# A joint unit order for the first batch and the front of the second in a fused retention and Fourier-mix kernel

## The chip, the cores and the metric

The kernel runs on one core of a Trainium2 chip. A core has five engines that run their own instruction streams and meet at semaphores: PE (TensorE, matrix products into PSUM), DVE (VectorE), ACT (ScalarE), POOL (GpSimd) and SP (SyncE, which here only issues DMA transfers). POOL also issues transfers, on a queue of its own that can convert fp32 to fp16. The metric is the device time of one execution in microseconds (us), as the median of several executions.

## The reference

Two layers follow one another. The first is a retention recurrence for 4 batches, 8 heads, 768 steps and head size 64; the second mixes the result with a two-dimensional Fourier transform and runs a normed MLP of width 2048.

```
for t in range(S):
    state = gamma * state + k[t] (outer) v[t]      # per batch and head
    y[t] = scale * q[t] @ state
x = y as (B, S, H * D)                             # 4 x 768 x 512
X = fft(fft(x, axis=1), axis=2)
u = x + real(X)
un = (u - mean(u)) / sqrt(var(u) + 1e-6)           # per row
out = u + relu(un @ w_ch1) @ w_ch2                 # 512 -> 2048 -> 512
```

## The kernel before

One batch after another goes through the same stages. The front of a batch is attention, folds, the two transform stages and the norm; its main part is the MLP.

*Attention.* The recurrence is cut into 6 chunks of 128 steps, and the heads are taken in four pairs. For a pair, q and k are cast to fp16 (k with its decay factor), transposed on PE, multiplied chunk by chunk to masked products (tile `atm`), and k with v gives chunk states (`s16`) that are chained on DVE. Output `y` is the masked product times v plus q times the state before the chunk; it is written to `x16` in fp16. For the first batch these are the small units `q0_unit` (L449), `kl_unit` and `vl_unit` (k and v loads on POOL's queue, L457 and L464), `k0_unit` (L472), `t0_unit` and `te_unit` (transposes and their copies), `am_unit` and `ae_unit` (products on PE, mask on DVE, L515 and L530), `kv0_unit`, `sc_unit`, `yi_unit`, `yx_unit` and `x0_unit`. For later batches larger units do the same: `cast_unit` (L414), `t_unit`, `a_unit`, `kv_unit` and `y_unit`, each with its matmuls and its evictions in one unit.

*Transform.* The sums and differences of mirrored rows and columns (`fold_s` L730, `fold_d` L747, `fold_e`) halve the work; stage 1 (`ps1`, `psA`, `psB`) multiplies by cosine and sine tables over the steps, stage 2 (`pq`) over the 512 features. For the first three row blocks of the first batch, `s2e_unit` (L958) works on PE with x added by `px_unit`; all other blocks go through `s2_unit` (L1025): products, a copy `qn` on ACT, two DVE combinations into `u`, two additions of x on POOL (L1072, L1074), row statistics on DVE (L1085) and the normed `un` on ACT (L1087). `unT_unit` transposes `un` on PE, for later batches by DMA.

*MLP.* 16 column blocks of the first product (`h_unit`, L1126; relu on ACT for the rows named in `ACT_ROWS`, else on DVE) are kept in `ht16` for 384 rows at a time; `ch_unit` (L1170) forms three blocks of 128 output rows from them, 16 matmuls each, and writes `out`. For the first 384 rows of the first batch, `h0_unit` (L1136, matmul L1143) does the first product in 12 groups of 16 matmuls of 128 columns.

*Loads.* SP issues four q loads at the start. The k and v loads of the first batch, the eight weight loads (`w1_unit`, `w2_unit`, 512 KB each in fp16) and the v loads of the second batch are issued by POOL. The second batch's q and k loads (`load_unit`, L163) are issued by SP with two added waits: for the seventh weight load (`w_dma[6]`) and for the last matmul of the eighth `h0_unit` (`lb[0]["mm"]`).

*Order.* `first_units` is a list written out by hand. Its units are emitted one by one, and `pin` ties every instruction to the one before it on its engine, so each engine runs them in list order. All that follows, from the second half of the first batch on, is given to `emit` (L1239) as streams of units with due times (`DM0`, `TS0`, `DA0`, `LD0` for the first batch, `DM1`, `TS1`, `DA1`, `LD1` for the others, in units of one batch); units are emitted by due time, and a planner may then move instructions on an engine, except that up to due time 0.05 all engines and up to 1.0 POOL are pinned, and that nothing up to 1.0 goes ahead of the hand-made list (`behind`). `filler(n)` puts n matmuls on PE whose result is not used.

Of the kernel before, what the change touches and what calls it, by code (L numbers as in the profile page):

```python
# [18 lines left out]
P = 128  # L19
# [11 lines left out]
LOADS = (('q', 0), ('q', 1), ('q', 3), ('q', 2))  # L31
# [3 lines left out]
DM0, DM1 = (0.120, 0.208, 0.265, 0.344), (0.004, 0.137, 0.232, 0.341)  # L35
TS0 = (0.249, 0.368, 0.406, 0.410, 0.479, 0.544, 0.680, 0.685)
# [3 lines left out]
HT0 = (0.655, 0.675, 0.673, 0.628)  # L40
NPE = 2
ACT_ROWS = ((2, 5, 6, 7, 8, 9, 10, 14), (0, 3, 6, 7, 9, 10, 11, 12, 14, 15), (2, 4, 5, 6, 7, 8, 10, 14))
# [3 lines left out]
def kernel(  # L46
# [116 lines left out]
    def load_unit(b, i, after=None):  # L163
        def run():
            h0 = 2 * PAIR_ORDER[i]
            for name, src in srcs.items():
                if b == 1 and name == "v":
                    continue
# [3 lines left out]
                dma = nc.sync.dma_start(t, src[b, h0:h0 + 2].rearrange(rows, p=P))  # L172
                if after is not None:
                    for x in (w_dma[after].ins, lb[0]["mm"].ins):
                        tc.add_manual_dep(dma.ins, x.name,
                                          mybir.DependencyInfo(mybir.DependencyClass.Sync,
                                                               mybir.DependencyReason.DATA),
                                          reason="loads in turn")
# [96 lines left out]
    def late_consts():  # L275
        with tc.issue_after(lb[0]["una"].ins):
            for h in range(H):
                nc.scalar.activation(maskp[:, h // 2, h % 2], maskf, AF.Copy, bias=0.0,
                                     scale=float(gam[h] ** (-P)))

# [26 lines left out]
    def eng_of(eng):  # L307
        return nc.vector if eng == "V" else nc.gpsimd
# [295 lines left out]
    def t_unit(b, i):  # L604
        def run():
            st = at[b, i] = {}
            kT = st["kT"] = tp.tile([P, NCH, P], f16, tag="kT", name="kT")
            if b >= NPE:
                qT = st["qT"] = qts[i % 2]
                nc.sync.dma_start_transpose(qT.rearrange("p h c t -> p (h c) t"),  # L610
                                            q16_of[b, i].rearrange("p h c d -> p (h c d)"))
                nc.sync.dma_start_transpose(kT, kd_of[b, i].rearrange("p c h d -> p (c h d)"))
                return
            qT = st["qT"] = qts[i % 2] if b else qts[i % 2][:, 0]
            for dst, src in ((qT, q16_of[b, i]), (kT, kd_of[b, i])):
                tq = ps_g.tile([P, NCH, P], f16, tag="g", name="tq", padded_shape=[P, 8, P])
                for c in range(NCH):
                    nc.tensor.transpose(tq[:, c, :], src[:, c].rearrange("p a b -> p (a b)"),
                                        ident16)
                if dst is qT:  # L620
                    for h2 in range(2 if b else 1):
                        rows = slice(D * h2, D * h2 + D) if b else slice(0, P)
                        dst = qT[rows, h2] if b else qT
                        (nc.scalar.copy if h2 == 0 or ON_ACT["q"][min(b, 2)] else nc.vector.tensor_copy)(
                            dst.rearrange("p c t -> p (c t)").rearrange(
                                "p (t c) -> p t c", c=NCH),
                            tq[rows].rearrange("p c t -> p t c"))
                else:
                    nc.scalar.copy(dst, tq)
        return run  # L630

    def a0_unit(b, i, half):
        def run():
            st = at[b, i]
            hp = PAIR_ORDER[i]
            if half == 0:
                st["atm"] = ap_.tile([P, NCH, 2, P], f16, tag="atm", name="atm")
            wk = [ps_g.tile([P, 3, P], f32, tag="g", name="wkA", padded_shape=[P, 4, P])
                  for _ in range(2)]
            for c3 in range(3):  # L640
                c = 3 * half + c3
                for h2 in range(2):
                    sl = slice(D * h2, D * h2 + D)
                    nc.tensor.matmul(wk[h2][:, c3, :], st["kT"][sl, c, :], st["qT"][sl, c, :],
                                     start=True, stop=True)
            for h2 in range(2):
                nc.vector.scalar_tensor_tensor(
                    out=st["atm"][:, 3 * half:3 * half + 3, h2, :], in0=wk[h2],
                    scalar=float(gam[2 * hp + h2] ** (-P)),
                    in1=maskf.unsqueeze(1).to_broadcast([P, 3, P]),  # L650
                    op0=ALU.mult, op1=ALU.mult)
        return run
# [483 lines left out]
    def h0_unit(kb, g):  # L1136
        def run():
            unT = lb[0]["unT"]
            psh = ps_pm.tile([P, 4, P], f32, tag="pm", name="psh0")
            for f in range(4):  # L1140
                fb = 4 * g + f
                for cb in range(4):
                    mm = nc.tensor.matmul(psh[:, f], w116[:, cb, fb * P:(fb + 1) * P],  # L1143
                                          unT[:, cb, kb * P:(kb + 1) * P],
                                          start=(cb == 0), stop=(cb == 3))
            lb[0]["n"] = lb[0].get("n", 0) + 1
            if lb[0]["n"] == 8:
                lb[0]["mm"] = mm
            dst = ht16[:, 4 * g:4 * g + 4, kb * P:(kb + 1) * P]
            if g % 2 == 0:  # L1150
                nc.scalar.activation(dst, psh, AF.Relu, bias=0.0, scale=-1.0)
            else:
                nc.vector.tensor_scalar(out=dst, in0=psh, scalar1=-1.0, scalar2=0.0,
                                        op0=ALU.mult, op1=ALU.max)
        return run

# [82 lines left out]
    def emit(streams):  # L1239
# [16 lines left out]
    late_consts()  # L1256
    streams = []
    for b in range(B):
        majors = []
# [64 lines left out]
```

## Time and profile before

| | us |
|---|---|
| median of 3 runs (251.27 to 251.73) | 251.46 |
| the profiled execution's own time | 250.45 |
| its span, first to last instruction | 248.7 |
| PE busy | 236.4 |
| DVE busy | 175.7 |
| ACT busy | 120.9 |
| POOL busy | 91.1 |
| last matmul ends, last store follows | 245.6 |

The profile records each instruction of one execution. A group of equal instructions stands as line, engine, operation, output<-inputs, shape and count, followed by the time that its engine sat idle before it and what ended that idle time. The page also cuts the span into 40 slices of 6.2 us each, in which a digit is the busy share in tenths, and lists the granted clock of PE in the same way. Windows views give busy times for any stretch. Waits views sum the idle time by who waited for whom. The chain of waits follows the last instruction back to what released it. Three more readings: 29 fillers (L156) run between 1.3 and 20.3 us; the transfers of the second batch's k took 10.84 us in that chain; weight loads landed 5.3 to 14.7 us after their issue.

### The profile page before, as it was taken

Reading aid. Unit: us, or ns where it says so; the run is one execution under the profiler, and the core shown is the slowest. Engines: PE = TensorE matmul, PEld = TensorE weight load, DVE = VectorE, ACT = ScalarE, POOL = GpSimd, SP = SyncE. Lnnn points to the kernel's source line nnn. Section 1 sums busy time; section 2 is a strip of 40 time slices with the busy share of each in tenths; the row PEclk is TensorE's granted clock in tenths of the full one; section 3 lists DMA queues with packets and bytes.
Section 4 is the critical chain, followed back from the end, with each engine's and each line's share of the span. In section 5 each row is a group of like instructions: output and inputs, shape, how many; then the busy total and the mean of one; then the engine's idle time right before and its main releaser. Section 6 shows DMA issues by size and latency. Waiting matters only on the chain.

```text
span 248.7 us, 5403 instructions
## 1 busy us (share of the span) xinstructions
PE 236.4 (95%) x2082; PEld 147.6 (59%) x2082; DVE 175.7 (71%) x420; ACT 120.9 (49%) x272; POOL 91.1 (37%) x152
## 2 busy tenths in 40 slices
PE   7897999996999997999999999999999999999994
PEld 2464999743766554665567546655567455445543
DVE  8999645688899878997787647896995747424112
ACT  7886564639686355563237523741248317202500
POOL 8999493154600037782000454780001305000000
PEclk9999599999999999999999999999999999999999
DMA  7999099999769314997989068997200241221012
GB/s 194 182 149 153 2 176 190 187 192 280 252 159 278 72 46 103 234 214 153 244 221 252 8 122 232 208 202 162 87 0 3 44 148 25 44 84 42 3 42 84
DMA packets 99210, 34.04 MB, mean 137 GB/s; under 512 B 89840, under 2 KB 96240, under 8 KB 99184
## 3 DMA queue, kind: packets, MB, share of 16 engines
q1 hardware_dynamic: 76336, 27.14, 45.8%
q0 software_dynamic: 22848, 6.55, 25.4%
q8 instruction: 16, 0.26, 0.4%
q14 instruction: 10, 0.08, 0.1%
HBM read 27.26 MB, written 6.29 MB: 135 GB/s over the span
## 4 chain that ended last, share of the span: by engine, by line
PE 69%; DVE 11%; POOL 8%; DMA 4%; ACT 3%; issue 3%; SPq 1%; POOLq 0%; ACTq 0%
PE psc L1170 26%; PE psh L1126 23%; DMA k<-in_k_dram 4%; PE psh L1143 4%; DVE atm L533 3%; PE wkA L662 3%; PE ps L873 2%; PE wkY L716 2%; PE wkY L712 2%; SPq L172 1%; POOL u L1074 1%; POOL u L1072 1%; DVE xab L741 1%; DVE bst L1085 1%; DVE u L1051 1%
## 5 line engine op out<-in xcount | busy, mean ns | idle before, releaser
L1170 PE MATMUL psc<-w,ht 128*128 128x512 f16 (+2 forms) x400 | 88.1, 370 | 0.0
L1126 PE MATMUL psh<-unT,w 128*128 128x384 f16 x448 | 83.1, 326 | 0.4 <-ACT ht L1130 0.2
L1170 PEld LDWEIGHTS <-ht 128*128 128x128 f16 x400 | 37.8, 98 | 37.9
L1126 PEld LDWEIGHTS <-w 128*128 128x128 f16 x448 | 42.1, 98 | 23.8 <-issue 1.5
L1072 POOL TENSOR_TENSOR u<-u,x 128x256 f32<-128x256 f32 x21 | 13.3, 635 | 106.6 <-DVE u L1051 93.3
L1130 ACT ACTIVATE ht<-psh 128x384 f16<-128x384 f32 x64 | 30.8, 490 | 42.1 <-PE psh L1126 41.6
L1174 DVE SCALAR_TENSOR_TENSOR ob<-psc,stats,u 128x512 f32<-128x512 f32 (+2 forms) x25 | 18.0, 725 | 27.0 <-PE psc L1170 26.5
L1132 DVE TENSOR_SCALAR ht<-psh 128x384 f16<-128x384 f32 x48 | 26.3, 550 | 7.9 <-PE psh L1126 7.5
L1087 ACT ACTIVATE un<-u,stats 128x512 f16<-128x512 f32 x21 | 15.1, 721 | 22.6 <-DVE stats L1086 14.8
L665 DVE TENSOR_TENSOR atm<-wkA,maskp 128x512 f16<-128x512 f32 x36 | 23.9, 684 | 2.5 <-PE wkA L662 2.5
L1085 DVE BATCH_NORM_STATS2 bst<-u 128x6 f32<-128x512 f32 x21 | 14.6, 694 | 8.8 <-POOL u L1074 8.6
L691 DVE SCALAR_TENSOR_TENSOR s<-s,gk,wkK 128x128 f16<-128x128 f16 x48 | 16.2, 338 | 2.2 <-ACT s L687 1.6
L724 ACT ACTIVATE x<-wkY,gexp 128x384 f16<-128x384 f32 x24 | 12.7, 580 | 6.3 <-PE wkY L716 6.1
L435 POOL TENSOR_SCALAR kd<-k,gexp 128x384 f16<-128x384 f32 x24 | 13.8, 585 | 4.7 <-DMA k<-in_k_dram 4.7
L1074 POOL TENSOR_TENSOR u<-u,x 128x256 f32<-128x256 f32 x21 | 13.3, 635 | 3.0 <-DVE u L1054 1.8
L662 PE MATMUL wkA<-qTz,kT 128*128 128x256 f16 x72 | 13.3, 273 | 0.1
L1046 ACT COPY qn<-pq 128x128 f32<-128x128 f32 x18 | 4.9, 273 | 13.2 <-PE pq L1044 12.6
L1143 PE MATMUL psh<-unT,w 128*128 128x128 f16 x192 | 11.2, 219 | 0.0
L156 PE MATMUL wps<-ht 128*128 128x512 f16 x29 | 10.0, 491 | 1.3 <-DVE ht L217 1.3
L1051 DVE SCALAR_TENSOR_TENSOR u<-pq,g,qn 128x256 f32<-128x256 f32 x18 | 8.5, 473 | 3.6 <-PE psh L1126 2.5
L1143 PEld LDWEIGHTS <-w 128*128 128x128 f16 x192 | 10.9, 98 | 0.1
L662 PEld LDWEIGHTS <-kT 128*128 128x128 f16 x72 | 6.8, 98 | 5.7 <-DMA kT<-kd 0.6
(187 smaller groups left out, 341.4 us busy)
## 6 DMA issues: line engine op xcount, KB each, us to landing
q<-in_q_dram SPq DMA_DIRECT2D x16, 384.0 KB, 5.3
out_dram<-ob SPq DMA_DIRECT2D x23, 256.0 KB, 2.3
k<-in_k_dram SPq DMA_DIRECT2D x12, 384.0 KB, 4.9
w<-in_moe_w_ch_dram POOLq DMA_DIRECT2D x8, 512.0 KB, 9.0
v<-in_v_dram SPq DMA_DIRECT2D x8, 384.0 KB, 4.7
v<-in_v_dram POOLq DMA_DIRECT2D x8, 192.0 KB, 10.9
k<-in_k_dram POOLq DMA_DIRECT2D x4, 192.0 KB, 6.9
unT<-un SPq DMA_TRANSPOSE x15, 2.4
```

What stands on the lines that cost most here:

```text
L662: mm = nc.tensor.matmul(wk[:, c2], st["kT"][:, c, :], st["qT"][:, :, c, :], start=True, stop=True)
L665: nc.vector.tensor_tensor(out=st["atm"][:, 2 * part:2 * part + 2], in0=wk, in1=maskp[:, PAIR_ORDER[i]].unsqueeze(1).to_broadcast([P, 2, 2, ...
L691: nc.vector.scalar_tensor_tensor(out=s16[:, c], in0=s16[:, c - 1], scalar=gk2[:, hp:hp + 1], in1=wk[:, c - c0], op0=ALU.mult, op1=ALU.add)
L1072: nc.gpsimd.tensor_tensor(out=u[:, kb, 0:256], in0=u[:, kb, 0:256], in1=x[:, kb, 0, 1:257], op=ALU.add)
L1074: nc.gpsimd.tensor_tensor(out=u[:, kb, 256:512], in0=u[:, kb, 256:512], in1=x[:, kb, 1, 257:1:-1], op=ALU.add)
L1085: nc.vector.bn_stats(bst, u[:, kb, :])
L1126: nc.tensor.matmul(psh, w116[:, cb, fb * P:(fb + 1) * P], unT[:, cb, rt * 384:(rt + 1) * 384], start=(cb == 0), stop=(cb == 3))
L1130: nc.scalar.activation(ht16[:, fb, :], psh, AF.Relu, bias=0.0, scale=-1.0)
L1132: nc.vector.tensor_scalar(out=ht16[:, fb, :], in0=psh, scalar1=-1.0, scalar2=0.0, op0=ALU.mult, op1=ALU.max)
L1143: mm = nc.tensor.matmul(psh[:, f], w116[:, cb, fb * P:(fb + 1) * P], unT[:, cb, kb * P:(kb + 1) * P], start=(cb == 0), stop=(cb == 3))
L1170: nc.tensor.matmul(psc[:, c0:c1], ht16[:, fb, rb3 * P:(rb3 + 1) * P], w216[:, fb, c0:c1], start=(fb == 0), stop=(fb == NFB - 1))
L1174: nc.vector.scalar_tensor_tensor(out=ob[:, c0:c1], in0=psc[:, c0:c1], scalar=lb[b]["st"][:, rb, 3:4], in1=lb[b]["u"][:, rb, c0:c1], op0=AL ...
```

## The change

The list of `first_units` now runs to the end of the second batch's front. It holds 498 units in a new order, and ten groups of fillers between them. What the planner placed before from `h0_unit` on (the first batch's second half, the second batch's attention, folds, transform stages and first norms) is cut into small units of the same list: matmuls and their evictions apart, with the engine of most evictions written into the list (`"A"`, `"V"` or `"P"`). All of it is pinned on all engines. `emit` starts at the second batch's MLP; nothing due before 1.2 goes ahead of the list, and POOL is no longer pinned there.

In the front of the first batch the order is new as well: the first k load on POOL stands behind the first q cast; the seven first weight loads follow one another closely, with casts, mirror copies and one fold between them; 38 fillers instead of 29 with other groupings; some casts, copies and folds on other engines. The q loads of the start come in the order 0, 2, 1, 3. The second batch's q and k loads wait for `w_dma[6]` only, and three of its four v loads stand later in POOL's order. Loads of the third batch are in the list too, ahead of the first batch's stores on SP. The per-head masks (`late_consts`) become four units. `ACT_ROWS` gives ACT 9, 12 and 10 relu rows instead of 8, 10 and 8, and the due times of the later batches are new.

```diff
-LOADS = (('q', 0), ('q', 1), ('q', 3), ('q', 2))
+LOADS = (('q', 0), ('q', 2), ('q', 1), ('q', 3))
-DM0, DM1 = (0.120, 0.208, 0.265, 0.344), (0.004, 0.137, 0.232, 0.341)
-TS1 = (-0.040, -0.020, 0.048, 0.585)
-DA0, DA1 = (0.068, 0.080, 0.173, 0.203, 0.315, 0.321), (0.063, 0.067, 0.063, 0.158, 0.168, 0.189)
-LD0, LD1 = (0.172, 0.226), (-0.370, 0.140)
+DM1 = (-0.053, 0.122, 0.081, 0.252)
+TS1 = (-0.154, 0.065, 0.056, 0.572)
+DA1 = (0.063, 0.085, 0.12, 0.141, 0.204, 0.295)
+LD1 = (-0.128, 0.184)
+BEHIND = 1.2
-ACT_ROWS = ((2, 5, 6, 7, 8, 9, 10, 14), (0, 3, 6, 7, 9, 10, 11, 12, 14, 15), (2, 4, 5, 6, 7, 8, 10, 14))
+ACT_ROWS = ((0, 2, 5, 6, 7, 9, 10, 11, 13), (0, 1, 4, 5, 7, 8, 9, 10, 11, 12, 14, 15), (0, 2, 4, 5, 7, 8, 10, 11, 13, 14))
...
                 if after is not None:
-                    for x in (w_dma[after].ins, lb[0]["mm"].ins):
-                        tc.add_manual_dep(dma.ins, x.name,
+                    tc.add_manual_dep(dma.ins, w_dma[after].ins.name,
...
+    def ck1(i, h2, eng):
+        def run():
+            h = 2 * PAIR_ORDER[i] + h2
+            if h2 == 0:
+                kd_of[1, i] = kp.tile([P, NCH, 2, D], f16, tag="kd16", name="kd16")
+            dst, src = kd_of[1, i][:, :, h2, :], in_of["k", 1, i][:, h2]
+            if eng == "A":
+                nc.scalar.activation(dst, src, AF.Copy, bias=0.0, scale=gkd[:, h:h + 1])
+            else:
+                eng_of(eng).tensor_scalar(out=dst, in0=src, scalar1=gkd[:, h:h + 1], scalar2=1.0,
+                                          op0=ALU.mult, op1=ALU.mult)
+        return run
...
+    def hm(fb):
+        def run():
+            psh = lb[0]["h", fb] = ps_pm.tile([P, 384], f32, tag="pm", name="psh",
+                                              padded_shape=[P, DM])
+            for cb in range(4):
+                nc.tensor.matmul(psh, w116[:, cb, fb * P:(fb + 1) * P], lb[0]["unT"][:, cb, 384:768],
+                                 start=(cb == 0), stop=(cb == 3))
+        return run
+
+    def he(fb, eng):
+        def run():
+            relu(eng, ht16[:, fb, :], lb[0]["h", fb])
+        return run
...
     def first_units():
-        return [parity_a, kl_unit(0), icoln_unit, trig(3, 0, "A"), zero_unit, kl_unit(1), ...]
+        return [
+            mask_unit, trig(1, 0, "V"), zero_unit, parity_a, icoln_unit, edge_unit,
+            trig(0, 0, "V"), trig(0, 1, "P"), trig(3, 0, "A"), ident_unit, trig(2, 0, "V"),
+            trig(4, 0, "V"), trig(4, 1, "V"), trig(2, 1, "V"), q0_unit(0), trig(2, 2, "V"),
+            filler(4), t0_unit(0, 0), kl_unit(0), trig(0, 2, "V"), t_act(0, 2), trig(3, 1, "V"),
+            filler(10), t0_unit(0, 1), trig(4, 2, "V"), t_act(4, 2), t_act(2, 2),
...
+            ae_unit(2, 0, 1), ae_unit(2, 0, 0), w1_unit(2), w1_unit(3), mir_s(0, "P"),
+            w2_unit(0), te_unit(3, 0, "A"), ae_unit(2, 1, 0), x0_unit(1, 0, "A"),
...
+            mir_d(1, "A"), csn_unit(0, "A"), load_unit(1, 0, 6, "qk"), x0_unit(3, 0, "A"),
...
+            h0m(2, 3), h0e(2, 3, "A"), cm(0, 1), tm1(0, 0), b0_unit(0), h0e(2, 1, "V"),
+            s2x(0, 3, 1, "V"), cm(2, 0), cm(2, 1), cm(2, 2), kvm(0, 0), s2b(0, 3),
+            s2n(0, 3, "P"), kvm(0, 1), kvc(0, "A"), s2u(0, 4), s2x(0, 4, 0, "V"), ck1(1, 0, "A"),
...
+            cm(5, 3), ce(3), uTe(1, 0, "A"), ce(5), uTe(1, 1, "A"), uTe(1, 2, "A"),
+            load_unit(2, 2, None, "v"), load_unit(2, 3),
+        ]
...
         for e in ev:
             e[3]()
-            if e[0] < 1.0:
+            if e[0] < BEHIND:
                 behind()
-                pin(None if e[0] < 0.05 else ["Pool", "GpSimd"])
...
-    for b in range(B):
+    for b in range(1, B):
```

The new small units and what they stand for: `cq1` and `ck1` cast the second batch's q and k, `tm1` and `te1` transpose and copy, `am1` and `ae1` form and mask the products, `kvm`, `kvc` and `kve` the states, `yx1`, `yi1` and `xe1` the attention output; `fe1`, `s1m`, `s1e` and `s1r` are the transform's first stage; `s2m`, `s2q`, `s2u`, `s2x`, `s2b` and `s2n` are `s2_unit` in six parts, `uTm` and `uTe` are `unT_unit` in two; `h0m` with `h0e`, `hm` with `he` and `cm` with `ce` are the MLP's products and evictions.

More of the change, by code (lines that the diff above doesn't have):

```diff
@@ L629, in run @@
                     nc.scalar.copy(dst, tq)
[L630 to L651, printed above, removed]
         return run
@@ L1134, in h_unit @@
         return run
[L1136 to L1155, printed above, removed]
     psc_of = {}
@@ new lines, in tm1, with run @@
+    def tm1(i, part):
+        def run():
+            if part == 0:
+                at[1, i] = dict(kT=tp.tile([P, NCH, P], f16, tag="kT", name="kT"), qT=qts[i % 2])
+            tq = at[1, i]["tq", part] = ps_g.tile([P, NCH, P], f16, tag="g", name="tq",
+                                                  padded_shape=[P, 8, P])
+            src = (q16_of, kd_of)[part][1, i]
+            for c in range(NCH):
+                nc.tensor.transpose(tq[:, c, :], src[:, c].rearrange("p a b -> p (a b)"), ident16)
+        return run
@@ new lines, in te1, with run, am1 @@
+    def te1(i, h2, eng):
+        def run():
+            st = at[1, i]
+            if h2 == 2:
+                any_copy(eng, st["kT"], st["tq", 1])
+                return
+            rows = slice(D * h2, D * h2 + D)
+            any_copy(eng, st["qT"][rows, h2].rearrange("p c t -> p (c t)").rearrange(
+                "p (t c) -> p t c", c=NCH), st["tq", 0][rows].rearrange("p c t -> p t c"))
+        return run
+    def am1(i, part):
+        def run():
+            st = at[1, i]
+            if part == 0:
+                st["atm"] = ap_.tile([P, NCH, 2, P], f16, tag="atm", name="atm")
+            wk = st["wk", part] = ps_g.tile([P, 2, 2, P], f32, tag="g", name="wkA")
+            for c2 in range(2):
+                c = 2 * part + c2
+                a_of[1, i] = nc.tensor.matmul(wk[:, c2], st["kT"][:, c, :], st["qT"][:, :, c, :],
+                                              start=True, stop=True)
+        return run
@@ new lines, in ae1, with run, kvm @@
+    def ae1(i, part):
+        def run():
+            st = at[1, i]
+            nc.vector.tensor_tensor(
+                out=st["atm"][:, 2 * part:2 * part + 2], in0=st["wk", part],
+                in1=maskp[:, PAIR_ORDER[i]].unsqueeze(1).to_broadcast([P, 2, 2, P]),
+                op=ALU.mult)
+        return run
+    def kvm(i, half):
+        def run():
+            st = at[1, i]
+            kd, v16 = kd_of[1, i], v16_of[1, i]
+            c0, n = ((0, 3), (3, 2))[half]
+            wk = st["kv", half] = ps_g.tile([P, 3, P], f32, tag="g", name="wkK",
+                                            padded_shape=[P, 4, P])
+            for c in range(c0, c0 + n):
+                nc.tensor.matmul(wk[:, c - c0, :], kd[:, c].rearrange("p a b -> p (a b)"),
+                                 v16[:, :, c, :], start=True, stop=True)
+        return run
@@ new lines, in he, with run, cm @@
+    def he(fb, eng):
+        def run():
+            relu(eng, ht16[:, fb, :], lb[0]["h", fb])
+        return run
+    def cm(rb, part):
+        def run():
+            if part == 0:
+                lb[0]["c", rb] = ps_pm.tile([P, DM], f32, tag="pm", name="psc")
+            r = rb % 3
+            for fb in range(4 * part, 4 * part + 4):
+                nc.tensor.matmul(lb[0]["c", rb], ht16[:, fb, r * P:r * P + P], w216[:, fb, :],
+                                 start=(fb == 0), stop=(fb == NFB - 1))
+        return run
@@ L1255 @@
     base.update(tails)
[L1256 removed]
     streams = []
[L1258 to L1263 removed]
+    for b in range(1, B):
+        majors = [h_unit(b, 0, fb) for fb in range(NFB)]
         majors.append(rstd_unit(b, 0))
```

356 lines of the change are left out of this document (322 added, 34 removed).

## The prediction

> **What bounds the kernel now.** I first read the page's shares and its 40 slices, to find which engine is busy and where it is not.
>
> ```profile
> PE 236.4 (95%) x2082; PEld 147.6 (59%) x2082; DVE 175.7 (71%) x420; ACT 120.9 (49%) x272; POOL 91.1 (37%) x152
> ...
> PE   7897999996999997999999999999999999999994
> ...
> DVE  8999645688899878997787647896995747424112
> ...
> PEclk9999599999999999999999999999999999999999
> DMA  7999099999769314997989068997200241221012
> ```
>
> PE is the bound: only 12.3 us of the 248.7 us span are not PE work, and a reordering can win little outside the first 16 slices (100 us). In slice 4 (24.9 to 31.1 us) the granted clock is 0.5 and DMA stands at 0. Next I cut the windows view at four events: first key transposes (9.82, where PE had waited for a key load), first matmul of the first MLP (33.44, L1143), end of the second batch's front (97.55, L1044 on g16r), last matmul (245.6). Columns: length, then busy time of PE, PEld, DVE, ACT, POOL with counts, clock, DMA share, GB/s.
>
> ```profile
> 9.82:33.44 23.62, 21.44 (x341) 16.51 (x342) 20.54 (x40) 17.55 (x37) 19.54 (x32) 0.86 1.16 109
> 33.44:97.55 64.11, 60.11 (x634) 41.53 (x632) 48.89 (x123) 39.11 (x82) 23.31 (x36) 1.00 0.95 177
> 97.55:245.60 148.05, 147.04 (x1081) 86.36 (x1078) 97.64 (x225) 57.04 (x137) 39.34 (x66) 1.00 0.53 121
> ```
>
> The first stretch is a latency chain in which DVE is 20.5 of 23.6 us busy. The second holds 4.0 us of PE idle time (64.11 - 60.11), the third 1.0. The waits view for PE from 33 to 98 us names the 4.0, and the chain of waits shows the largest of them from its root:
>
> ```profile
> PE tq L618 <- POOL kd L435: 2.3, 2, 1.1
> PE pst L1113 <- ACT un L1087: 1.0, 1, 1.0
> PE wkY L712 <- ACT kT L629: 0.4, 2, 0.2
> PE ps L922 <- DVE xg L913: 0.2, 1, 0.2
> ```
>
> ```profile
> 46.78 0.36 SPq L172
> ...
> 50.31 10.84 DMA k<-in_k_dram
> 61.23 1.16 POOL kd L435 x2
> 62.44 0.51 PE tq L618 x6
> ```
>
> SP could not issue the second batch's loads before 46.8 us: it waited 43.9 us for the seventh weight load. The keys then came 10.5 us later (casts at 57.29), the next pair's at 61.23, and both held PE. Last, one-microsecond windows around the clock's fall:
>
> ```profile
> 22.00:23.00 1.00, 0.42 (x9) 0.17 (x3) 1.00 (x2) 0.49 (x1) 1.00 (x1) 1.00 1.24 202
> 23.00:24.00 1.00, 0.48 (x9) 0.38 (x11) 1.00 (x1) 0.50 (x1) 1.00 (x2) 0.90 0.77 130
> 24.00:25.00 1.00, 0.60 (x13) 0.31 (x7) 1.00 (x2) 0.34 (x1) 0.35 (x1) 0.50 0.19 31
> 26.00:27.00 1.00, 1.00 (x16) 1.00 (x14) 0.56 (x2) 0.62 (x2) 0.00 (x0) 0.50 0.00 0
> ```
>
> From 20.5 to 24 us PE was about two thirds busy (the windows of 20 and 21 us read 0.94 and 0.88), waiting on folds and masked products; after that the clock was 0.50 until 30.7. PE was full from 25.2 to 30.7, so 5.5 us at half clock cost about 2.7.
>
> **The change part by part.** The PE instruction list keeps all its real matmuls; only fillers grow, from 29 to 38. Nine more at 0.22 us (four took 1.03 at full clock, less the last one's tail) are 2.0 us, all ahead of the first MLP, where PE waits for DVE anyway: nothing, and 2.0 if that cover were gone. So the sum has three terms, one per stretch.
>
> *Term 1, start of the first MLP (33.44 before).* The first key load moves on POOL's queue from 1.5 us to behind three memsets, a mask, the identity and the first q cast. That cast needs q, which had landed by 4.62; POOL's own ops before it end near 4 us; so the cast runs 4.5 to 5.3 and the key load is issued 5.3 to 6.35 (1.03 each). Before, keys shared the transfers with all four q loads (8.3 us from issue to landing, the worst of four; best 5.6). The q loads have a 4 us lead now. By the best row the keys land at 10.9, by my reading that q is through before them (key data at about 145 GB/s, the windows from 9 to 16 us, 0.2 MB in 1.4 us) at 9.3. I take 9.3, since DMA moved 263 to 326 GB/s in each microsecond from 2 to 6, which carries 1.57 MB of q by 7.7; 10.9 goes to the range. From there DVE is followed by its list: 4 key casts (0.75), 3 transposed copies (0.5), 16 masked products (0.54), 4 scans (0.75), one fold of 774 and one of 390 elements (0.6 and 0.35, by 384 elements in 0.32), parity 0.2. That is 17.5 without waits, against 16.7 before (9.82 to 26.56): two more key casts, one more copy and a larger fold come in, and the fold that took 1.97 beside POOL's folds (L741) should cost 0.35, since POOL's fold now ends before it. Two folds at 0.5 end at 27.8. Then PE: s1 12 matmuls at 0.1, s1a and s1b 1.4, px and s2e 3.0, with three DVE and ACT hand-overs: first MLP at 33.7 at full clock. It is +0.3. But one px and two s2e groups that followed 33.44 now precede it: 0.46 us less remains. Term 1: -0.2. Ends: -1.0 (DVE ready earlier) and +2.7 (the clock falls again).
>
> *Term 2, first MLP and second front (64.1 us, 60.1 of it PE).* The weights' seven loads are issued from about 15 to 26 us instead of 15.5, 18.7, 29.8 to 34.5, so the hole at slice 4 closes. First-batch keys and values end near 19 us (1.57 MB at 145); 7 x 0.524 MB follow at 171 GB/s (the row: five weights from 29.75 to 46.77, 1.7 us off for latency) to 195 (the rate inside 32 to 40 us): landing between 37.8 and 40.5. The wait on the eighth unit's matmul (lb[0]["mm"]) is gone; it was past by 41 us, so it costs nothing now. SP issues the second batch's q and k then, 6 to 9 us earlier, and three of four v loads move behind, out of their way. PE reaches the second batch's first key product at 33.7 + 17.3 of PE work = 51 us, and its second pair's key transposes at 54. Keys issued at 40 land by 50.5 and 54.4 at the old pace, less some 3 us for 0.6 MB of values that no longer share: the 2.3 us wait goes. The 1.0 at L1113 falls to about 0.4: the list puts 7 quarter products (0.86 each) ahead of the first transpose and one between, while s2m, qn, u, add, statistics and un for the last block take 8 us. What is new: every engine now keeps list order through 98 us, where the planner had moved PE work past a late operand. Behind each waiting cast on POOL stand other casts and the row norms (s2n "P"), behind ck1 on ACT the copies te1, and PE waits for both. I bound the idle time from both sides by rows: 0.6 (only the last transposes and the old 0.2) and 4.0 (as now, other places). The middle, 2.3: term 2 is -1.7. DVE's units in the new list, each at its row, sum to 52 us of some 62 (48.9 of 64 before): no bound, though near.
>
> *Term 3, the rest (148 us, 1.0 idle).* New due times, and 9, 12 and 10 instead of 8, 10 and 8 relu rows on ACT: five rows in 48 change engine per batch pair, ACT 0.49 for DVE 0.55, both with slack (57 and 98 us of 148). The first cast of the next batch is due later, so PE asks for it later and the 0.4 wait for POOL v (L443) should go. -0.2; ends -0.8 and +1.5 (as many waits again as stretch two has per 60 us).
>
> Sum: -0.2 - 1.7 - 0.2 = -2.1 from the profiled execution's 250.45 us (span 248.7 and 1.7 around it), 248.4; the three runs' median is 251.46, 1.0 above it, so 249.4 for runs.
>
> Two rules that bear on this. Weight loads issued while DVE was 6.00 of 6.00 us busy (15.5 and 18.7 us) took POOL 0.75 to 0.82 us, as at 30 us. The Trainium skill, "SBUF — State Buffer", section "Who interferes with whom", says that DVE's two-port operations lock GpSimd out, so that a DMA issued from GpSimd waits for its descriptors; seven loads under a full DVE would then be late. The rows show no such delay, and the sum keeps 0.77 per issue.
>
> The Trainium skill, "TensorE: Matmul & The Clock Gate", section "HAM oscillation — how this bites in real kernels", asks for idle gaps above some 3 us before the clock falls. The longest gap here was 1.1 us and the clock fell: the measurement decides, and the risk of a second fall stays.
>
> **The rivals.**
> - *The second batch's loads come late (the other side).* If weight seven lands after 41.7 us (keys at 14.4 us after issue less 3 against PE at 53), POOL's and ACT's casts stand, everything queued behind them stands too, and PE idles one us per us: from 43.8 on it eats the 2.1. For: landing to issue of weights was up to 14.7 us. Against: my 40.5. At 45, midway to the old 46.8, PE loses 3.3: 252.7.
> - *The clock falls again.* More fillers speak against it, small matmuls at 64 columns and a DVE-bound front for it. Price 2.7: 252.1.
> - *The front is won but the idle time moves:* term 2 at 4.0, no gain in term 3: 251.2, no change.
> - *More is won:* term 1 at -1.0, term 2 at -3.4, term 3 at -0.5: 246.6.
> - *It does not do what it says:* w2_unit(3) and one v load still share with the second batch's loads, so the pause could persist; its time is the first rival's and its chance is counted there.
>
> **How the numbers follow.** Forecast 0.49 (248.2 to 250.9), more won 0.14, no change 0.13, clock 0.10, late loads 0.14. What a measurement can tell from no change is about 0.2%, 0.5 us. Faster: 0.49 + 0.14 + a quarter of no change = 0.66. Within: the greater part of no change, 0.08. Slower: clock, late loads and the last sixth = 0.26. The range 246.6 to 252.6 leaves out half of the late loads and the best part of "more won".
>
> **What would show it.** First MLP matmul near 33.7 us; PEclk 9 in slice 4; DMA without a zero before slice 7; SP's wait for w ending near 40; no PE wait for ck1 or cq1 casts; PE idle about 2.3 between first MLP and the second front's end, that end near 95.5. A clock of 5 in slices 3 to 5, a second key landing after 54, or new PE waits above 4 us in that stretch make me wrong.

## The result, and the profile after

| | before | after |
|---|---|---|
| median of 20 runs each | 250.62 | 251.92 |
| ratio after / before, 95% interval | | 1.0047 (1.0026 to 1.0067) |
| the profiled execution's own time | 250.45 | 251.60 |
| its span | 248.7 | 249.5 |

The changed kernel is 0.5% slower. The forecast was 249.4 us and faster; the range of 246.6 to 252.6 holds the time, the sign is wrong. One run of the 20 lies far off on each side (272.48 us before; 485.75 us after, in which a matmul of 384 columns took 559 ns instead of 326), the ratio leaves both out, and the profile shown for the changed kernel is that of another execution, e13 below.

The page of the changed kernel, the same rows as before the change:

```profile
PE 234.9 (94%) x2091; PEld 146.5 (59%) x2091; DVE 177.1 (71%) x424; ACT 122.4 (49%) x277; POOL 88.3 (35%) x143
...
PE   7699799999999999997799999889999999999994
...
DVE  8699879999999888766795738876894647323012
...
PEclk9999999999999999999999999999999999999999
DMA  6999999958998019998995179996200241121012
```

The clock's hole in slice 4 is gone, and so is the zero of the transfers there. In PE's row the low digits have moved: from slices 9 and 15 before (inside the two fronts) to slices 18 and 19 now (112 to 125 us, behind the second front), and weaker ones to slices 25 and 26. The windows view of the changed kernel, cut at the same events (first key transposes, which start at 9.70 here, 0.1 us behind the first edge; first MLP; end of the second front) and at two more, the start of the 48 matmuls of the second and of the third batch's first `ch_unit` groups:

```profile
9.59:34.05 24.46, 21.95 (x361) 15.79 (x362) 21.63 (x48) 18.52 (x41) 20.49 (x26) 1.00 1.61 184
34.05:92.49 58.44, 58.16 (x628) 41.74 (x627) 53.63 (x128) 34.98 (x75) 21.13 (x29) 1.00 0.82 154
92.49:138.39 45.90, 42.54 (x366) 26.67 (x365) 34.11 (x81) 21.73 (x52) 12.96 (x22) 1.00 0.93 198
138.39:192.79 54.40, 52.20 (x415) 31.36 (x413) 39.17 (x93) 24.23 (x58) 18.99 (x33) 1.00 0.54 117
192.79:246.30 53.51, 53.07 (x302) 28.16 (x299) 21.00 (x43) 16.66 (x39) 6.85 (x12) 1.00 0.18 55
```

and the last three of these stretches in the kernel before:

```profile
97.55:139.39 41.84, 41.47 (x368) 26.90 (x366) 34.36 (x83) 19.75 (x49) 14.11 (x24) 1.00 0.96 205
139.39:192.11 52.72, 52.47 (x417) 31.29 (x414) 40.25 (x95) 22.40 (x55) 18.88 (x33) 1.00 0.54 120
192.11:245.60 53.49, 53.10 (x303) 28.17 (x300) 23.04 (x47) 14.88 (x35) 6.35 (x11) 1.00 0.18 55
```

Read the left edges. The second front ends at 92.49 instead of 97.55: a lead of 5.1 us. At the next mark it is 1.0 (138.39 against 139.39), at the one after it is a debt of 0.7 (192.79 against 192.11), and that stays to the end. So the front won more than twice what was forecast, and two stretches behind it gave all of it back: 4.1 us (45.90 - 41.84) and 1.7 us (54.40 - 52.72). PE's three largest waits behind the second front in the changed kernel (total, times, longest):

```profile
PE wkA L638 <- DMA qTz<-q16z: 3.0, 2, 1.5
PE psh L1102 <- DVE ht L1108: 1.0, 1, 1.0
PE wkY L692 <- DVE atm L641: 0.7, 1, 0.7
```

The first line is 3.0 of the 4.1 us: twice 1.5 us for the transposed q of the third batch (at 115.9 and 122.6 us). The other two lie in the stretch that lost 1.7. For the first line, SP's queue in the changed kernel (start, length):

```profile
94.07 0.41 SPq L170 DMA_DIRECT2D v<-in_v_dram  x1
94.58 0.79 SPq L170 DMA_DIRECT2D q<-in_q_dram  x1
95.46 1.41 SPq L170 DMA_DIRECT2D k<-in_k_dram  x1
98.82 0.37 SPq L170 DMA_DIRECT2D v<-in_v_dram  x1
99.29 3.04 SPq L608 DMA_TRANSPOSE qTz<-q16z  x1
```

and in the kernel before:

```profile
96.36 1.55 SPq L610 DMA_TRANSPOSE qTz<-q16z  x1
98.02 1.55 SPq L612 DMA_TRANSPOSE kT<-kd  x1
...
100.26 0.42 SPq L172 DMA_DIRECT2D v<-in_v_dram  x1
```

Before, the third batch's first q was transposed 1.2 us ahead of the end of the second front, and its last loads came behind. Now the four last loads (`load_unit(2, 2, None, "v"), load_unit(2, 3)`, the last entries of the list) stand in front, and the transpose is issued 6.8 us behind the end of the second front. POOL's queue shows who waits for whom:

```profile
89.42 0.99 POOL L430 TENSOR_SCALAR q16z<-q 128x384 f16<-128x384 f32 x2
...
97.81 0.98 POOL L430 TENSOR_SCALAR q16z<-q 128x384 f16<-128x384 f32 x2
...
104.59 0.98 POOL L430 TENSOR_SCALAR q16z<-q 128x384 f16<-128x384 f32 x2 [2.44 <-DMA qTz<-q16z]
```

and in the kernel before the first of these casts is:

```profile
95.35 0.99 POOL L432 TENSOR_SCALAR q16z<-q 128x384 f16<-128x384 f32 x2
```

The first pair's casts were done at 92.3 in the changed kernel, and only SP's queue kept them from being transposed. The last v load needs an input buffer that the second pair's q cast (97.81) gives back; SP stood 1.9 us for it, and the first pair's transposes stood behind it. The third pair's cast (104.59) writes the buffer that the first pair's transpose reads, waited 2.44 us for it, and its own transpose came late for PE. Of the two other profiles of the changed kernel one (e14, 251.00 us) shows two such waits too, the other (e1, 252.15 us) one of 2.2 us and a fall of the clock behind it.

### The profile page after: what moved, and what is told of

Same layout as the page of the kernel before. It is cut to its first block, busy times and chain, and to the rows that moved or that the text cites. A ratio compares the mean times of both kernels' runs of the same rounds, so it can differ in the third digit from the quotient of the medians.

```text
span 483.6 us, 5412 instructions
## 1 busy us (share of the span) xinstructions
PE 479.2 (99%) x2091; PEld 233.0 (48%) x2091; DVE 182.8 (38%) x424; ACT 124.8 (26%) x277; POOL 88.0 (18%) x143
## 4 chain that ended last, share of the span: by engine, by line
PE 99%; DVE 0%; issue 0%
PE psh L1102 28%; PE psc L1125 28%; PE psc L1479 9%; PE psh L1464 5%; PE psh L1449 5%; PE wps L155 4%; PE wkA L638 2%; PE ps L849 2%; PE pq L1020 1%; PE tq L1187 1%; PE pq L940 1%; PE wkY L692 1%; PE wkA L1209 1%; PE wkY L688 1%; PE wkK L657 1%; PE ps L1305 1%
## 5 line engine op out<-in xcount | busy, mean ns | idle before, releaser
L1102 PE MATMUL psh<-unT,w 128*128 128x384 f16 x384 | 142.0, 559 | 0.0
L1125 PE MATMUL psc<-w,ht 128*128 128x512 f16 (+2 forms) x304 | 139.6, 655 | 0.0
L1102 PEld LDWEIGHTS <-w 128*128 128x128 f16 x384 | 54.2, 144 | 66.0 <-issue 63.1
L1125 PEld LDWEIGHTS <-ht 128*128 128x128 f16 x304 | 44.5, 150 | 79.1 <-issue 77.2
L1479 PE MATMUL psc<-w,ht 128*128 128x512 f16 x96 | 47.8, 681 | 0.0
L1048 POOL TENSOR_TENSOR u<-u,x 128x256 f32<-128x256 f32 x15 | 9.6, 637 | 202.7 <-DVE u L1027 199.3
L1108 DVE TENSOR_SCALAR ht<-psh 128x384 f16<-128x384 f32 x32 | 17.8, 556 | 58.9 <-PE psh L1102 58.9
L1464 PE MATMUL psh<-unT,w 128*128 128x384 f16 x64 | 25.0, 566 | 0.0
L1479 PEld LDWEIGHTS <-ht 128*128 128x128 f16 x96 | 14.3, 154 | 22.1 <-issue 21.7
L1449 PE MATMUL psh<-unT,w 128*128 128x128 f16 x192 | 23.8, 328 | 0.0
L1449 PEld LDWEIGHTS <-w 128*128 128x128 f16 x192 | 21.7, 148 | 2.5 <-issue 0.5
L1438 ACT ACTIVATE ht<-psh 128x384 f16<-128x384 f32 (+1 forms) x24 | 12.2, 529 | 34.5 <-PE psh L1449 21.0
L155 PE MATMUL wps<-ht 128*128 128x512 f16 x38 | 19.0, 655 | 1.3 <-DVE ht L214 1.3
L1464 PEld LDWEIGHTS <-w 128*128 128x128 f16 x64 | 9.1, 148 | 9.1 <-issue 8.2
```

The costliest lines, as they stand in the source:

```text
L155: nc.tensor.matmul(wps, wz[:, 0:P], wz, start=True, stop=True)
L1102: nc.tensor.matmul(psh, w116[:, cb, fb * P:(fb + 1) * P], unT[:, cb, rt * 384:(rt + 1) * 384], start=(cb == 0), stop=(cb == 3))
L1108: nc.vector.tensor_scalar(out=ht16[:, fb, :], in0=psh, scalar1=-1.0, scalar2=0.0, op0=ALU.mult, op1=ALU.max)
L1125: nc.tensor.matmul(psc[:, c0:c1], ht16[:, fb, rb3 * P:(rb3 + 1) * P], w216[:, fb, c0:c1], start=(fb == 0), stop=(fb == NFB - 1))
L1438: nc.scalar.activation(dst, src, AF.Relu, bias=0.0, scale=-1.0)
L1464: nc.tensor.matmul(psh, w116[:, cb, fb * P:(fb + 1) * P], lb[0]["unT"][:, cb, 384:768], start=(cb == 0), stop=(cb == 3))
```

## The experiments

Each time is the median of that kernel's runs (one run for e1, e13 and e14), each ratio is to the kernel before, run on the same chip. Names such as e4 stand for the runs in the order in which they were made.

**Where the loss lies** (e1, the changed kernel as it is).

> The changed kernel once more, unedited, for a profile of an execution whose PE clock is not at half rate throughout. Theory A (my first and second stretch were too hopeful): first MLP matmul well after 33.7 us, or PE idle time of 4 us and more between it and the end of the second front, span 249 to 250. Theory B (the front came as forecast, the later batches lost it): first MLP near 33.7, second front's end near 95.5, and PE idle time of 3 us and more in the stretch after it where it was 1.0.

252.15 us. First MLP at 34.02, second front's end at 92.59, PE idle 0.29 us between them: B, with more won in the front than B asked. What followed therefore looked behind the front, with two theories: Q, SP's queue (the loads in front of the transposes), and D, the new due times and relu rows.

**Loads and due times, one at a time (e2, e3) and together (e4).** The last four loads leave the end of `first_units` for the streams of `emit`; the constants go back to those of the kernel before.

```diff
-            load_unit(2, 2, None, "v"), load_unit(2, 3),
...
+            else:
+                streams.append(([load_unit(2, 2, None, "v"), load_unit(2, 3)], 1.0, 1.14))
```

> Only change to the new kernel: the last loads of the third batch (v of its third pair, q, k, v of its fourth) are no longer the last entries of the list, but are given to the due-time emitter behind the first transposes of that batch on SP. Theory Q (SP's queue holds the third batch: those loads wait for buffers that casts of the second pair free, and the DMA transposes of the first pair stand behind them): the first q transposes are issued near 94 us instead of 99.4, PE's 2.2 us wait for them near 115 us and the half clock behind it are gone, time 3 to 5 us below the changed kernel's 252, so 247 to 249. Theory D (the new due times and relu rows lose the time): the transposes may come earlier, but the time stays within 1 us of 252.

250.23 us, ratio 0.9987 (0.9964 to 1.0011). The first q transposes went at 94.4, as Q said, but PE then waited 1.5 us for the third batch's keys, and the waits for `atm` and `ht` near 160 us stayed: 1.7 us won of the 3 to 5 expected.

```diff
-DM1 = (-0.053, 0.122, 0.081, 0.252)
+DM1 = (0.004, 0.137, 0.232, 0.341)
...
```

> The new kernel with the due times (DM1, TS1, DA1, LD1) and the relu rows of the kernel before; list and SP order untouched. Theory Q: the first q transposes are still issued near 99 us, PE still waits about 2 us for them; only the 1.3 us that the last two batches lost (wait for atm 0.7, for ht 0.9 near 161 and 164 us) come back: 250.5 to 251.5. Theory D: the whole loss of 6 us after the second front goes, 246 to 247.

(With TS1, DA1, LD1 and ACT_ROWS as with DM1.) 253.38 us, ratio 1.0097 (1.0058 to 1.0135). Both theories missed: with the loads still in front the old due times do not help (the interval touches that of the changed kernel), with PE waits of 2.4 us for kT, 1.2 for POOL's v and 1.5 for relus.

> Both edits together. Theory Q with the 1.3 us of the due times beside it: 246 to 247.5, better than each alone. Theory D: as with the due times alone, 246 to 247. If a third cause holds the third batch (third transposes, casts on POOL, unT transposes on SP), both stay above 249.

246.63 us, ratio 0.9846 (0.9824 to 0.9868): both edits together make the front's gain arrive. Moving the loads is worth 1.7 us with the new due times (251.92 to 250.23) and 6.8 with the old ones (253.38 to 246.63); the old due times cost 1.5 us with the loads in front and win 3.6 with them behind. (By the ratios, which take out the difference between chips, the four are 1.5, 6.3, 1.3 and 3.5 us.) Neither is the cause alone. SP's queue in this version:

```profile
94.13 1.59 SPq L608 DMA_TRANSPOSE qTz<-q16z  x1
95.82 1.56 SPq L610 DMA_TRANSPOSE kT<-kd  x1
97.43 0.57 SPq L170 DMA_DIRECT2D v<-in_v_dram  x1
98.18 2.65 SPq L608 DMA_TRANSPOSE qTz<-q16z  x1
```

Its second front ends at 92.47 (as in the changed kernel), the two later marks are 135.08 and 187.63, and no PE wait behind the front is above 0.2 us: of the lead of 5.1 us, 4.3 and 4.5 are left at the two marks.

The same marks show where each edit acts. The lengths in us of the two stretches behind the second front, from one profile each:

| | loads in front | loads behind |
|---|---|---|
| new constants | 45.90 and 54.40 (the changed kernel) | 44.39 and 54.62 (e2) |
| old constants | 49.56 and 52.53 (e3) | 42.61 and 52.55 (e4) |

The second of the two stretches follows the constants alone; in the first both act. Of e3's 49.56, 1.7 us is a fall of the granted clock around its wait of 2.4 us. Three of its four runs have a mean clock of 0.993 and take 253.3 to 253.5 us; the one at 1.000 takes 251.56, no more than the changed kernel.

**The new due times in the kernel before** (e5; same constants, its own list; the third batch's loads keep their old due times).

> The kernel before with the new due times and relu rows for the later batches; its own hand-made list, and its own due times of the loads of the third batch. Theory D: slower than before by 2 us or more. Theory Q: the new due times cost at most the 1.3 us of the last two batches here too, so 0 to 1.3 us above the kernel before.

252.92 us, ratio 1.0088 (1.0055 to 1.0122), 2.2 us slower by the ratio: here D's number holds and Q's is too small. PE waits: 1.4 us for `atm`, 0.9 for `ht`. The new constants cost time in the old list too. Its second front ends at 97.29 (97.55 before) and the two marks behind it are 140.88 and 195.03, so 1.8 and 1.4 us are lost in the two stretches behind the front and none ahead of it.

**Half a dose of the load order** (e10; base: the 246.6 us version).

```diff
+            load_unit(2, 2, None, "v"), load_unit(2, 3, None, "qk"),
...
+                streams.append(([load_unit(2, 3, None, "v")], 1.0, 1.14))
```

> As the version with old due times (246.6 us with all four last loads behind the first transposes, 253.4 with all four in the list ahead of them), but with v of the third pair and q, k of the fourth left in the list and only the last v load behind the transposes. Theory Q says that SP stands at that last v load, for the buffer that the second pair's casts free: the first q transposes then go at about 97 us, between 94.1 and 98.7, and the time lies between, 247.5 to 250. If it is the transfers of the loads themselves that delay the transposes: still 252 or more.

249.06 us, ratio 0.9945 (0.9924 to 0.9966), first q transposes at 97.19: in between, in place and in time. The load that waits for a buffer is part of the delay, the three ahead of it another part.

**Which of the constants** (base: the 246.6 us version; e6 with the new `ACT_ROWS` alone, e7 with the new `DM1` alone).

> The version with the loads behind the transposes and all due times of the kernel before, but with the new relu rows (9, 12, 10 on ACT). Against the same with the old rows (246.6 us). If the rows cost the later batches their time (ACT fuller, its sqrt later, DVE's reciprocal and relus behind it): 249 to 250. If the due times do: 246.3 to 247.2.

> As the 246.6 us version, but with the new DM1 alone (the second half's transform blocks of the later batches and their transposes on SP asked for earlier). Theory M (DM1 does it: the third normed block waits on ACT for a buffer that a transpose on SP has yet to read, the square root stands behind it, DVE's reciprocal waits about 2.2 us, relus and masks behind that; and on SP the same transposes stand ahead of the keys'): 249 to 250.3, with PE waits for atm of 0.7 and for ht of 0.9 again. If TS1 or DA1 are the cause: 246.3 to 247.5.

Rows alone: 249.40 us, ratio 0.9941 (0.9912 to 0.9970). `DM1` alone: 251.04 us, ratio 1.0016 (0.9981 to 1.0051), more than expected. So both cost, and not additively, since all new constants together cost 3.6. With `DM1` the wait is not the one that Theory M put first: PE waits 2.3 us for the third batch's kT. On SP the second batch's unT transposes now go at 102.8 and 108.9, between the third batch's transposes, and its third q transpose goes at 110.8 instead of 105.4. With the rows, ACT stands 5.9 us in two waits of the next kind, and PE waits 1.6 us for a relu on ACT. By the marks, against the 246.6 us version, the rows cost 0.2 and 2.6 us in the two stretches, and `DM1` 4.2 and 1.1. Of the 4.2, 1.7 is a fall of the clock, and this profile (252.69 us) is one of the longest of its ten runs.

**ACT's wait.** In the changed kernel the third normed block of a half has to wait on ACT for a buffer:

```profile
162.60 0.72 ACT L1063 ACTIVATE un<-u,stats 128x512 f16<-128x512 f32 x1 [2.83 <-DMA unT<-un]
163.23 0.28 ACT L1076 ACTIVATE stats<-stats,epsT 128x3 f32<-128x3 f32 x1
```

and DVE stands behind ACT's square root:

```profile
163.54 0.18 DVE L1078 RECIPROCAL stats<-stats 128x3 f32<-128x3 f32 x1 [2.16 <-ACT stats L1076]
163.64 0.53 DVE L1108 TENSOR_SCALAR ht<-psh 128x384 f16<-128x384 f32 x1
```

The relu behind the reciprocal is the one that PE waited 1.0 us for. ACT's wait itself is not new: the kernel before has it too, at the same block.

```profile
165.02 0.72 ACT L1087 ACTIVATE un<-u,stats 128x512 f16<-128x512 f32 x1 [3.02 <-DMA unT<-un]
```

What is new is that DVE stands behind it. DVE's waits for the square root behind the second front (total, times, longest), before and after:

```profile
DVE stats L1102 <- ACT stats L1100: 1.1, 3, 0.5
DVE stats L1078 <- ACT stats L1076: 5.1, 4, 2.2
```

So the wait for the buffer alone costs PE nothing; what the new order queues behind it does. e8 takes the wait away by a third buffer (base: e2's version, 250.2 us, new due times):

```diff
+    unp = pool("unp", 3)
...
-            un = up.tile([P, 2, 257], f16, tag="un16", name="un16").rearrange(
+            un = unp.tile([P, 2, 257], f16, tag="un16", name="un16").rearrange(
```

> As the version with new due times and loads behind the transposes (250.2 us), with three buffers instead of two for the normed blocks un. Theory M: ACT no longer stands 2.9 us for the transpose, DVE's reciprocal no longer 2.2; the PE waits for atm (0.7) and ht (0.9) go in the later batches, time 1.5 to 3 us less, 247.2 to 248.7. If ACT's or DVE's work itself is the cause: 249.7 to 250.7.

248.07 us, ratio 0.9900 (0.9866 to 0.9934): 2.2 us less, inside Theory M's range. The wait for `ht` is gone, but the one of 0.7 for `atm` that M expected to go is left. The profiled execution (250.23 us) has a wait of 2.0 us for kT and a fall of the clock, so it is not typical; the last two stretches read 45.92 and 53.47 in it, against 44.39 and 54.62 in e2, and only the second gain, 1.2 us, is seen there. With the loads left in the list (e15) it does not help:

> The changed kernel with three buffers for un, its last loads left in the list. Theory M: only the waits of the later batches behind ACT go (0.7 and 0.9 us near 160 to 165), the third batch's wait for its q transposes stays: 250 to 251. If the transposes of un hold the third batch as well (they stand on SP ahead of the third pair's): 247.5 to 249.5.

251.69 us, ratio 1.0041 (1.0011 to 1.0070), a miss: the wait for `ht` is gone, but the third unT transpose now goes on SP ahead of the third batch's third q transpose (113.2 instead of 112.0), PE's wait there is 3.1 us and the clock falls.

**What the list needs of the weights.** Base: the 246.6 us version. In e9 `w2_unit(2)`, the seventh weight, moves beside the eighth; in e11 the tie of the second batch's loads is taken out.

```diff
-            yi_unit(2, 1), w2_unit(2), filler(4), ...
+            yi_unit(2, 1), filler(4), ...
+            w2_unit(2), w2_unit(3), px_unit(2), load_unit(1, 0, 6, "qk"), ...
```

> As the 246.6 us version, with the seventh weight issued beside the eighth (about 32 us instead of 25), so that the second batch's q and k loads leave SP near 42 to 44 us instead of 37.5. The prediction's threshold is 41.7 us, from which PE loses one us per us: 0.5 to 2.5 us slower, 247 to 249. If the front has more slack than that (first keys cast at 45 and used at 52 in the 246.6 us version): within 0.4 of 246.6. If early loads are where the front's 5 us come from: 250 or more.

245.93 us, ratio 0.9795 (0.9754 to 0.9835). Issued some 6 us later (31.5 us instead of 25), the weight landed at most 1.4 us later: SP's loads left at 38.83 instead of 37.47. The threshold of 41.7 us was not reached, so it stays untested. The first MLP starts at 33.3 us here instead of 34.0; the interval of the ratio overlaps that of the 246.6 us version.

```diff
-load_unit(1, 0, 6, "qk"), ...
+load_unit(1, 0, None, "qk"), ...
```

> As the 246.6 us version, with the tie of the second batch's q and k loads to the seventh weight taken out: SP issues them as soon as buffers are free, from about 10 to 25 us on, among the first batch's k and v and the weights. If the tie matters: the first batch's values or the weights come later, the first MLP starts 1 us or more after 34.0, time 247.6 or more. If transfers have room there: 246.2 to 247.

258.81 us, ratio 1.0352 (1.0315 to 1.0388). PE's waits, and the granted clock, in this version:

```profile
PE tq L494 <- DMA k<-in_k_dram: 4.9, 1, 4.9
PE wkK L546 <- DMA v<-in_v_dram: 4.6, 2, 2.8
```

```profile
PEclk9955799999999999999999999999999999999999
```

SP issues the second batch's loads between 2.9 and 19.4 us, the first batch's k and v come late, the clock falls, and the first MLP starts at 45.8. The tie is worth 12 us.

**The best of it** (e12, the 245.9 us version with the third buffer).

> The 245.9 us version (seventh weight beside the eighth, loads behind the transposes, old due times and rows) with three buffers for un. ACT still stands 2.3 to 2.8 us twice for a transpose there, but PE waits 0.2 us for it at most: by the PE waits a gain of 0 to 0.4, 245.5 to 246.2. If ACT's standing costs what it costs with the new due times: 243.5 to 244.5.

245.47 us, ratio 0.9802 (0.9779 to 0.9825), at the edge of what PE's waits let expect. It has the lowest median here, 2.0% below the kernel before; its interval overlaps that of e9, so that the third buffer adds anything here is not shown.

**The changed kernel twice more** (e13, e14).

> The changed kernel unedited once more. In the profiled execution of the first look PE's clock was halved for 3.4 us behind its 2.2 us wait, but 17 of 19 timed executions had a mean clock of 0.999 or 1.0 and took as long, 251 to 252.5. Theory Q with the wait alone: without the fall the wait for the third pair's transposes is still 1.5 to 2.2 us, batch two's second half starts near 137.5 instead of 139.4 us, time near 250.5. If another wait takes the fall's place: 251.3 to 252.5 with PE idle 1.5 us more, which the waits view names.

> The same once more, so that an execution without the fall is seen even if one of the two has it: 250.5 if the wait is all there is, 251.3 to 252.5 if another wait of about 1.5 us stands in its place.

251.60 us (the profile shown above) and 251.00 us, which lies between the two times expected for e14. Neither has the fall; each has a second wait of 1.5 us for the fourth pair's q transpose in its place (at 122.6 and 122.1 us). So the fall is not what made the kernel slow: late transposes cost 2.5 to 3.9 us in any of the three profiles.

## Why the prediction was wrong

*Term 1* was right in kind and 0.35 us off: first MLP at 34.05 (forecast 33.7), keys at PE at 9.7 (9.3), clock 1.00 through the front. Work moved ahead of the mark makes up for much of the 0.6 us that the mark lies later.

*Term 2* was right in mechanism and too small. SP's wait for the seventh weight ended at 39.3 (forecast 37.8 to 40.5), and no PE wait for a cast of q or k is left. But PE's idle time between first MLP and the second front's end is 0.28 us (58.44 - 58.16), where 2.3 was chosen from ends of 0.6 and 4.0. The front ends at 92.49, not 95.5. The choice in the middle came from the fear that pinned engines would stand behind late operands; in this order they don't. PE also counts 1.95 us less busy time than before (58.16 against 60.11), of which 0.46 was in the forecast; the rest is not accounted for. (The 64 matmuls `psh` of 384 columns count 12.5 us instead of 13.9, but that says nothing on gaps: they stand in 13 runs instead of 23, and each run counts the tail of its last matmul once, 0.33 us for one matmul and 0.81 for four.)

*Term 3* is the step that failed: "-0.2; ends -0.8 and +1.5". It measured +5.8 (4.06, 1.68 and 0.02 in the three stretches behind the front). Three things were wrong in it.
- It did not price the loads of the third batch that the list puts ahead of the transposes on SP. The part ahead of the prediction says that these loads stand ahead of the first batch's stores on SP; that holds for eight of the twelve. The last four, which its diff shows at the end of the list, stand behind the stores, right ahead of the transposes. SP's transposes were in the trace, with 1.2 us between the first of them and the front's end. A front that ends 5 us earlier needs these transposes 5 us earlier; it got them 2.9 us later (99.29 against 96.36). e4 and e10 show it.
- "The first cast of the next batch is due later, so PE asks for it later": that cast ran at 89.4 us, 5.9 earlier than before (95.35). Its transpose, not the cast, was late.
- It took the new due times and rows for harmless because ACT and DVE had slack on average (57 and 98 of 148 us). e5 shows some 2 us for them in the old list, e6 and e7 name rows and `DM1`. Slack in sum did not help where the order put a relu on DVE behind a square root on ACT, that behind a normed block, and that behind a transfer.

The upper end of the term, +1.5, was also too low by its own rule, "as many waits again as stretch two has per 60 us": stretch two has 4.0 us of idle time in 64.1, which is 3.7 per 60 us and 9.2 over the 148 us of the term.

*The rivals.* "The front is won but the idle time moves" (251.2) came nearest in kind, but it left the idle time inside the front; it moved past its end. Late loads and a second fall of the clock did not happen in the front. That the price of the fall, 252.1, is nearest to the measured time is chance: 17 of the 19 runs near the median have a mean clock of 0.999 or 1.0. The sum by measured terms: 5.06 us won up to the second front's end, 5.76 lost behind it, 0.7 us later at the last matmul; the profiled executions' own times differ by 1.15 and the medians by 1.30.

*Luck.* That the range holds the time is luck. The front won 3.2 us more than forecast (5.06 against 1.9), the rest lost 6.0 more (5.76 against -0.2), and the base of three runs, 251.46, was 0.8 above the median of 20.

*What stays open.* In the stretch from 92.49 to 138.39, 3.0 of the 4.06 us are idle time; the other 1.07 is PE time counted busy for nearly the same matmuls (42.54 against 41.47), which no view names. Not followed up was why the old due times do not help with the loads in front, nor what the front's order, fillers and closer weights each gave.

## What to carry to other kernels

When a stage gets faster, list what the next stage needs from each queue, with the time at which it now needs it, and price every issue that stands in front of it, above all one that waits for a buffer. An average slack of an engine says nothing of an order on it: follow the chain from a waiting instruction to what is queued behind it. And test two suspects together as well as one at a time: each edit alone here would have been called nearly worthless or harmful, both together made the kernel 1.5% faster.

## What the runs showed of the hardware

The granted clock after one wait of PE. In the profile of e1, PE had waited 2.21 us up to 116.75; the clock column reads 0.60, 0.50, 0.50, 0.69:

```profile
117.00:118.00 1.00, 1.00 (x7) 0.47 (x5) 0.84 (x2) 0.00 (x0) 0.00 (x0) 0.60 0.85 193
118.00:119.00 1.00, 1.00 (x9) 0.87 (x8) 0.88 (x3) 0.00 (x0) 0.00 (x0) 0.50 0.34 78
119.00:120.00 1.00, 1.00 (x5) 0.39 (x3) 1.00 (x3) 0.27 (x1) 0.00 (x0) 0.50 1.24 283
120.00:121.00 1.00, 1.00 (x16) 0.50 (x14) 0.99 (x3) 0.00 (x0) 0.00 (x0) 0.69 1.25 176
```

That is 1.7 us of full-clock work lost (0.40 + 0.50 + 0.50 + 0.31), as long as 3.4 us at half clock. The clock column lacks the same 1.7 us around single waits of 1.98, 2.28, 2.29, 2.37 and 3.08 us (e8, e5, e7, e3, e15), and nothing around waits of 1.51 to 1.61 us (e2, e6, e13, e14), of 1.84 us (e1, at 9.6 us) and of 1.90 us (e5, at 63.2 us). In e5 the fall is at 11 us, in the first batch's front; in e15 it begins before the wait has ended. So here a wait of 2 us cost nearly twice its length and one of 1.9 only itself, and times near that edge vary from run to run. With `DM1` alone, the four runs with a mean clock of 0.993 or less took 251.9 to 252.7 us, the six at 0.998 or more 249.8 to 251.2.

The Trainium skill, "TensorE: Matmul & The Clock Gate", section "HAM oscillation — how this bites in real kernels", puts the edge at gaps of some 3.4 us. Here it lay between 1.90 and 1.98 us, and 3.4 us is how long the fall lasted. The length of one gap is not the whole rule: in the kernel before, the clock fell at 24 us with no gap above 1.1 us near it, behind 3.5 us (20.5 to 24) in which PE was busy for 2.2.
